# Fused cosformer attention and quick-GELU MLP on one core: d_ff units dealt by fours, w_in in three tiles, w_out in 8 KB pieces, and k^T v of the next batch set behind the last group of the first product

## The chip, the cores and the metric

The kernel runs on one core of one Trainium2 chip, in one launch. The metric is the device time of a run in microseconds (us). The times given before are 295.08, 295.93 and 295.89 us, median 295.89 us. The execution that the profiler recorded took 295.09 us; from its first to its last instruction it spans 293.4 us. The granted TensorE clock in it is 0.997 of full speed.

## The reference

For each of 8 batches and 8 heads (sequence 576, head dimension 64) the reference computes a linear attention, then puts the heads side by side and runs a two-layer MLP with 512 inputs and 2048 hidden units (d_ff). Cut to what matters:

```python
def phi(x, c, s):                      # c, s: cos and sin of pi/2 * position / S
    r = np.maximum(x, 0.0)
    return np.concatenate([r * c, r * s], axis=-1)
q_p, k_p = phi(q, cos_w, sin_w), phi(k, cos_w, sin_w)
kv = np.einsum('bhsf,bhsd->bhfd', k_p, v)
num = np.einsum('bhsf,bhfd->bhsd', q_p, kv)
den = np.einsum('bhsf,bhf->bhs', q_p, k_p.sum(axis=2))[..., None] + 1e-06
x = (num / den).transpose(0, 2, 1, 3).reshape(B * S, H * D)     # 4608 x 512
h = x @ w_in                                                    # 512 x 2048
g = h * (1.0 / (1.0 + np.exp(-1.702 * h)))
out = g @ w_out                                                 # 2048 x 512
```

The order in which the 2048 hidden units are numbered does not matter to the result, as long as w_in's columns and w_out's rows are numbered alike.

## The kernel before

**The MLP.** The hidden units are cut into 16 groups of 128 (`fc` 0 to 15). The first product of a batch, `mm1(b, fc)` (L281, matmuls on L273), makes one group for 512 of the batch's 576 tokens: four matmuls, one for each 128 rows of w_in (`kc`). The stationary operand (the weights that TensorE loads ahead of a matmul) is a slice of w_in, 128 columns that lie side by side in SBUF; the moving operand is x transposed. ScalarE applies the GELU from PSUM to a tile `g` (L278). The second product, `mm2(b, t, lo, hi)` (L317, matmuls on L322), goes the other way round: for each of four blocks of 128 tokens, `g` is the stationary operand and rows of w_out move, over the groups `lo` to `hi`. ScalarE copies the result out (L326), and GpSimd's queue stores it (L329).

**The last 64 tokens of each batch** are kept apart in `xt`. For batches 0 and 1 they are done together (`mm1_tail_first`, L290, called for b = 0 and b = 1): two calls for each batch, 32 matmuls of 64 columns on L294 in each call, 128 in all, each with its own load of 128 columns of w_in. For the six later batches they wait for the end (`mm1_tails`, L298, 64 matmuls of 384 columns on L301).

**`start_block`** (L342) opens batches 0 and 1: its first four groups are done in pieces of 128 tokens, as soon as these are there, so that 128 of the matmuls on L273 have 128 columns; each loads its own 128 columns of w_in.

**The attention** of the next batch is woven into the MLP of this one. `trig` (L140, VectorE on L147) makes `kr`, the features of k; `vcopy` (L162, VectorE on L168) makes `vt`, v in bf16; `trig_q` and `qturn_dma` make the features of q and transpose them by DMA. `kv_mm` (L203, L208) multiplies k^T v in 72 small matmuls, `kv_evac` (L211, L213) copies the result to SBUF (`kvs`) on VectorE, and `num_mm` and `num_div` (L217 and L225) use it, one block of tokens between two pieces of `mm2`.

**Order.** The schedule is written out by hand: each engine takes its instructions in the order in which the program names them, and waits where one is not ready. In the loop over batches from 1 (L460) the next batch's `trig_q` come at the first group, its `trig`, its `vcopy` and the loads of the batch after it (`load_next`, on SyncE's queue) at the second; and ahead of group 15 stand these lines:

```python
            if nb is not None and fc == 15:
                kv_open()
                kv_mm(0, 4, vt_rhs, 0, 65)
                kv_evac(0, 4)
            mm1(b, fc)
```

For b = 1 the two `mm1_tail_first` calls (L482, L483) and `mm2(1, 4, 0, FC)` (L484) follow the loop over the groups; then, as for every batch, `mm2` of the four token blocks, with the next batch's `num_mm` after each eight matmuls. Batch 1's own k^T v stands in the stage of batch 0 (L437 to L439), which the change does not touch.

**Weights.** w_in is one tile of 128 x 4 x 2048 bf16, filled by four DMAs of 512 columns each (L118); w_out is one tile filled by four DMAs of four groups each (L127). All eight are issued by GpSimd's queue, which also converts from float32. In HBM a run of 512 columns of w_in is 2 KB; so is a row of w_out. Between these loads the same queue issues batch 1's k, q and v (L413 to L419). A DMA of this queue waits for the eighth before it, since eight semaphores are used in turn.

Of the kernel before, what the change touches and what calls it, by code (L numbers as in the profile page):

```python
# [10 lines left out]
BF16 = mybir.dt.bfloat16  # L11
# [8 lines left out]
def kernel(  # L20
# [9 lines left out]
    nc = tc.nc  # L30
    B, H, S, D = q.shape
    d_model = H * D
    d_ff = moe_w_in.shape[1]
    KC = d_model // 128
# [6 lines left out]
    one = ctx.enter_context(tc.tile_pool(name="one", bufs=1))  # L41
# [13 lines left out]
    def src_of(src, b, i0=0, i1=NI):  # L55
        return src[b, 2 * i0:2 * i1].rearrange("(i hh) (p j) d -> (hh p) i (j d)", hh=2, j=NS)
# [39 lines left out]
    qn0 = qn.rearrange("p c h f -> p (c h f)")[:, 0:NS * NI * 128].rearrange(  # L96
        "p (j i f) -> p j i f", j=NS, i=NI)
    qT = one.tile([128, H, 640], BF16, name="qT")
    w_in_sb = one.tile([128, KC, d_ff], BF16, name="w_in_sb")
    w_out_sb = one.tile([128, FC, d_model], BF16, name="w_out_sb")  # L100
    nc.gpsimd.memset(vt[:, :, :, 64:66], 1.0)
    nc.gpsimd.memset(qT[:, :, S:640], 0.0)


    win_r = moe_w_in.rearrange("(kc p) f -> p kc f", p=128)
    wout_r = moe_w_out.rearrange("(fc p) d -> p fc d", p=128)

    def load(t, src, b, eng=nc.gpsimd):
        eng.dma_start(out=t, in_=src_of(src, b))
# [4 lines left out]
        eng.dma_start(out=qf[0:64, 2048:2560].rearrange("p (h e) -> p h e", h=H),  # L114
                      in_=q[b, :, 512:S, :].rearrange("h p d -> p h d"))

    def load_win(f0, f1):
        nc.gpsimd.dma_start(out=w_in_sb[:, :, f0:f1], in_=win_r[:, :, f0:f1])  # L118

    def load_next(b):  # L120

        load_q(b, nc.sync)
        load(kf, k, b, nc.sync)
        load(vf, v, b, nc.sync)

    def load_wout(g):
        nc.gpsimd.dma_start(out=w_out_sb[:, ts(g, 4), :], in_=wout_r[:, ts(g, 4), :])  # L127

    gate = const.tile([1, 4], F32)
    nc.gpsimd.tensor_copy(gate[0:1, 0:1], kf[0:1, 0, 0:1])  # L130
    for i in (0, 2):
        nc.gpsimd.dma_start(out=vb[:, i:i + 2], in_=src_of(v, 0, i, i + 2))
    load_win(0, 512)
    load_win(512, 1024)
    nc.gpsimd.tensor_copy(gate[0:1, 1:2], vb[0:1, 3, 0:1])
    load_win(1024, 1536)
    load_win(1536, 2048)


    def trig(dst, src, j, act=False):  # L140
        i = src[:, :, ts(j, 64)]
        for cs, w in enumerate((cosw, sinw)):
            o = dst[:, j, :, ts(cs, 64)]
            if act:
                nc.scalar.activation(o, i, AF.Relu, scale=w[:, j:j + 1])  # L145
            else:
                nc.vector.tensor_scalar(o, i, 0.0, w[:, j:j + 1], op0=MAX, op1=MUL)  # L147

    def trig_q(c, act=False):
        n = 128 if c < 4 else 64  # L150
        if c < 4:
            i = qf[:, 0:2048].rearrange("p (h c d) -> p c h d", h=H, c=4)[:, c]
        else:
            i = qf[0:64, 2048:2560].rearrange("p (h d) -> p h d", h=H)
        for cs, w in enumerate((cosw, sinw)):
            o, sc = qn[0:n, c, :, ts(cs, 64)], w[0:n, NS + c:NS + c + 1]
            if act:
                nc.scalar.activation(o, i, AF.Relu, scale=sc)
            else:
                nc.vector.tensor_scalar(o, i, 0.0, sc, op0=MAX, op1=MUL)  # L160
# [27 lines left out]
    def qturn_dma(c):  # L188
        n = 128 if c < 4 else 64
        nc.sync.dma_start_transpose(out=qT[:, :, c * 128:c * 128 + n],  # L190
                                    in_=qn[0:n, c].rearrange("p h f -> p (h f)"))
# [3 lines left out]
    def kv_open(i0=0, i1=NI):  # L195
        t = pat.tile([128, 2, 512], F32, name="at")
        for i in range(i0, i1):
            st["kv", i] = t[:, :, ds((i - i0) * 65, 65)]
        st["ps", i0] = t[:, :, 0:(i1 - i0) * 65]
        if i0 == 0:  # L200
            st["kvs"] = small.tile([128, 2, NI, VW], BF16, name="kvs", bufs=2)

    def kv_mm(i0, i1, rhs, col, n):  # L203
        for i in range(i0, i1):
            for j in range(NS):
                for hh in range(2):
                    r = slice(hh * 64, hh * 64 + 64)
                    nc.tensor.matmul(st["kv", i][:, hh, ds(col, n)], kr[r, j, i, :], rhs(r, i, j),  # L208
                                     start=(j == 0), stop=(j == NS - 1))

    def kv_evac(i0, i1):  # L211
        o = st["kvs"][:, :, i0:i1, 0:65]
        nc.vector.tensor_copy(o, st["ps", i0].rearrange("p hh (i e) -> p hh i e", e=65))  # L213
# [23 lines left out]
    x = {}  # L237
# [29 lines left out]
    hp = {}  # L267

    def mm1_part(b, fc, t0, t1):
        if t0 == 0:  # L270
            hp[fc] = pmm.tile([128, MT], F32, name="mm")
        for kc in range(KC):
            nc.tensor.matmul(hp[fc][:, t0:t1], w_in_sb[:, kc, ts(fc, 128)], x[b][:, kc, t0:t1],  # L273
                             start=(kc == 0), stop=(kc == KC - 1))

    def gelu(fc):
# [4 lines left out]
    def mm1(b, fc):  # L281
        mm1_part(b, fc, 0, MT)
        gelu(fc)
# [3 lines left out]
    xt = one.tile([128, KC, B * 64], BF16, name="xt")  # L287
    gt = one.tile([128, FC, B * 64], BF16, name="gt")

    def mm1_tail_first(b, half):  # L290
        hps = pmm.tile([128, 8, 64], F32, name="mm")
        for f in range(8):
            for kc in range(KC):
                nc.tensor.matmul(hps[:, f], w_in_sb[:, kc, ts(half * 8 + f, 128)], xt[:, kc, ts(b, 64)],  # L294
                                 start=(kc == 0), stop=(kc == KC - 1))
        nc.scalar.activation(gt[:, ts(half, 8), ts(b, 64)], hps, AF.Gelu_apprx_sigmoid)

    def mm1_tails(fc):  # L298
        hps = pmm.tile([128, MT], F32, name="mm")
        for kc in range(KC):  # L300
            nc.tensor.matmul(hps[:, 128:B * 64], w_in_sb[:, kc, ts(fc, 128)], xt[:, kc, 128:B * 64],  # L301
                             start=(kc == 0), stop=(kc == KC - 1))
        nc.scalar.activation(gt[:, fc, 128:B * 64], hps[:, 128:B * 64], AF.Gelu_apprx_sigmoid)

# [3 lines left out]
    def rows(b, t):  # L308

        if t == 4:  # L310
            return [(64 * u, 64, out_j[NS - 1] if b + u == 1 else out[(b + u) * S - 64:(b + u) * S])
                    for u in range(2)]
        if b == 0:
            return [(64 * u, 64, out_j[2 * t + u]) for u in range(2)]
        return [(0, 128, out[b * S:b * S + 512].rearrange("(p c) d -> c p d", c=4)[t])]

    def mm2(b, t, lo, hi, c0=0, c1=d_model, last=False):  # L317
        if lo == 0:
            yp[b, t, c0] = pmm.tile([128, d_model], F32, name="mm")
        for fc in range(lo, hi):  # L320
            w = gT[fc][:, ts(t, 128)] if t < 4 else gt[:, fc, ts(b // 2, 128)]
            nc.tensor.matmul(yp[b, t, c0][:, c0:c1], w, w_out_sb[:, fc, c0:c1],  # L322
                             start=(fc == 0), stop=(fc == FC - 1))
        if hi == FC:
            ysb = ypool.tile([128, d_model], F32, name="ysb")
            nc.scalar.activation(ysb[:, c0:c1], yp[b, t, c0][:, c0:c1], AF.Identity)  # L326
            for p0, n, dst in rows(b, t):
                eng = nc.sync if last else nc.gpsimd
                eng.dma_start(out=dst[:, c0:c1], in_=ysb[p0:p0 + n, c0:c1])  # L329
# [130 lines left out]
    for b in range(1, B):  # L460
        nb = b + 1 if b + 1 < B else None
        f0 = 5 if b == 1 else 0
        for fc in range(f0, FC):
            if nb is not None and fc == f0:
                for c in range(5):
                    trig_q(c)
                    qturn_dma(c)
            if nb is not None and fc == f0 + 1:
                for j in range(NS):
                    trig(kr, kf, j)  # L470
                vcopy(0, 4)
                if nb + 1 < B:
                    load_next(nb + 1)
            if nb is not None and fc == 15:
                kv_open()
                kv_mm(0, 4, vt_rhs, 0, 65)
                kv_evac(0, 4)
            mm1(b, fc)
        if nb is not None:
            x_open(nb)  # L480
        if b == 1:
            mm1_tail_first(1, 0)  # L482
            mm1_tail_first(1, 1)  # L483
            mm2(1, 4, 0, FC)  # L484
        if nb is None:
            for fc in range(FC):
                mm1_tails(fc)
            for u in range(3, B, 2):
                mm2(u, 4, 0, FC)
        for t in range(4):  # L490
            last = nb is None and t == 3
            if last:
                mm2(b, t, 0, FC, 0, 256)
                mm2(b, t, 0, FC, 256, 512, last=True)
                continue
            mm2(b, t, 0, 8)
            if nb is not None and t < 3:
                num_mm(2 * t)
                num_div(2 * t)
                xturn_dma(nb, 2 * t)  # L500
            mm2(b, t, 8, 16)
            if nb is not None and t < 2:
                num_mm(2 * t + 1)
                num_div(2 * t + 1)
                xturn_dma(nb, 2 * t + 1)
# [30 lines left out]
```

## Time and profile before

| what | value |
|---|---|
| runs shown | 295.08, 295.93, 295.89 us; median 295.89 us |
| profiled execution | 295.09 us, span 293.4 us (1.7 us lie around the span) |
| TensorE (PE) busy | 283.6 us, 97% of the span |
| VectorE (DVE), ScalarE (ACT) busy | 123.7 us (42%), 128.6 us (44%) |
| matmuls of the second product, L322 | 592, 512 columns but for 32 of 256 |
| matmuls of the first product, L273 | 480 of 512 columns, 128 of 128 columns |
| tails of batches 0 and 1, L294 | 128 of 64 columns |
| tails of batches 2 to 7, L301 | 64 of 384 columns |
| w_in and w_out loads | 4 and 4 DMAs of 512 KB (as bf16), median 9.9 and 17.6 us from issue to landing |

In the profile PE is TensorE's matmul side and PEld its weight loads, which run beside the matmuls. Matmuls are pipelined, so the duration of one in the profile is longer than the distance to the next: 512 columns are listed with a mean of 379 ns, but four of them, one group, take 0.86 us. Where costs are worked out, distances from start to start are used and not durations.

### The profile page before, as it was taken

The numbers are of one execution on the slowest core, as the hardware profiler recorded it, in microseconds if no ns is written. First come the engines' busy times: TensorE is split into PE (matmuls) and PEld (weight loads), VectorE is DVE, ScalarE is ACT, GpSimd is POOL, SyncE is SP. The second block draws the span as 40 slices with busy tenths as digits, with TensorE's granted clock in tenths as the row PEclk, the third lists the DMA queues.
The fourth block names the chain that finished last, engine by engine and source line by source line (L and its number), as shares of the span: only waits on it lengthen the run. The fifth ranks groups of instructions, "written<-read, shape, count | busy, mean of one in ns | idle before, by whom it ended". The sixth has DMA issues, their size and how long they took to land.

```text
span 293.4 us, 6032 instructions
## 1 busy us (share of the span) xinstructions
PE 283.6 (97%) x2461; PEld 148.6 (51%) x2461; DVE 123.7 (42%) x355; ACT 128.6 (44%) x224; POOL 58.9 (20%) x71
## 2 busy tenths in 40 slices
PE   8889999989999999999999999999999999999992
PEld 3674556736544454445544554455445544564452
DVE  4764514871379037903691269225931510000000
ACT  7957724762115711572147214631364136771111
POOL 6351004100216001600151014301340110001211
PEclk9999999999999999999999999999999999999998
DMA  7999999999979965997499859895840430001311
GB/s 253 240 220 275 354 164 208 387 231 239 385 151 187 287 252 137 190 268 278 128 173 241 313 143 157 226 346 131 151 104 2 99 97 30 1 0 37 72 72 72
DMA packets 74795, 53.54 MB, mean 182 GB/s; under 512 B 52624, under 2 KB 65552, under 8 KB 74768
## 3 DMA queue, kind: packets, MB, share of 16 engines
q1 hardware_dynamic: 66160, 35.53, 49.2%
q0 software_dynamic: 8608, 17.63, 23.0%
q8 instruction: 19, 0.31, 0.4%
q14 instruction: 8, 0.07, 0.1%
HBM read 36.70 MB, written 9.44 MB: 157 GB/s over the span
## 4 chain that ended last, share of the span: by engine, by line
PE 87%; DMA 6%; DVE 3%; SPq 1%; ACT 1%; issue 0%; ACTq 0%
PE mm L322 41%; PE mm L273 33%; DMA kf<-in_k_dram 6%; PE at L208 4%; PE mm L301 4%; PE at L221 3%; DVE kr L147 2%; PE mm L294 1%; ACT kr L145 1%; PE mm L176 1%; DVE xn L233 1%; DVE vt L168 0%; SPq L190 0%; PE at L250 0%; SPq L114 0%
## 5 line engine op out<-in xcount | busy, mean ns | idle before, releaser
L322 PE MATMUL mm<-w_out_sb,g 128*128 128x512 bf16 (+1 forms) x528 | 117.4, 372 | 0.0
L273 PE MATMUL mm<-xT,w_in_sb 128*128 128x512 bf16 (+1 forms) x608 | 114.5, 345 | 0.0
L278 ACT ACTIVATE g<-mm 128x512 bf16<-128x512 f32 x128 | 75.5, 598 | 41.4 <-PE mm L273 41.4
L329 POOL DMA_DIRECT2D out_dram<-ysb x44 | 46.4, 1057 | 217.3 <-ACT ysb L326 217.1
L273 PEld LDWEIGHTS <-w_in_sb 128*128 128x128 bf16 x608 | 53.7, 98 | 55.3
L322 PEld LDWEIGHTS <-g 128*128 128x128 bf16 x528 | 49.2, 98 | 50.9
L326 ACT ACTIVATE ysb<-mm 128x512 f32<-128x512 f32 (+1 forms) x37 | 21.7, 585 | 107.7 <-PE mm L322 107.7
L233 DVE TENSOR_TENSOR xn<-at,inv 128x512 bf16<-128x512 f32 x40 | 27.7, 691 | 1.4
L147 DVE TENSOR_SCALAR kr<-kf,cosw 128x256 bf16<-128x256 f32 x68 | 23.5, 346 | 10.6 <-DMA kf<-in_k_dram 10.6
L213 DVE CAST kvs<-at 128x520 bf16<-128x520 f32 (+1 forms) x9 | 5.8, 642 | 49.1 <-PE at L208 49.0
L229 DVE TENSOR_SCALAR den<-at 128x8 f32<-128x8 f32 x40 | 6.7, 166 | 44.2 <-PE at L221 44.2
L147 DVE TENSOR_SCALAR kr<-kf,sinw 128x256 bf16<-128x256 f32 x68 | 23.7, 348 | 0.0
L221 PEld LDWEIGHTS <-qT 128*128 128x128 bf16 x320 | 14.6, 97 | 7.3
L160 DVE TENSOR_SCALAR qn<-qf,cosw 128x512 bf16<-128x512 f32 (+1 forms) x33 | 15.8, 479 | 3.3 <-DMA qf<-in_q_dram 3.3
L221 PE MATMUL at<-kvs,qT 128*128 128x65 bf16 x320 | 16.0, 193 | 0.0
L160 DVE TENSOR_SCALAR qn<-qf,sinw 128x512 bf16<-128x512 f32 (+1 forms) x33 | 15.8, 480 | 0.0
L322 PE MATMUL mm<-w_out_sb,gt 128*128 128x512 bf16 x64 | 14.1, 379 | 0.0
L208 PEld LDWEIGHTS <-kr 64*128 64x128 bf16 x648 | 10.3, 94 | 5.5 <-issue 4.5
L301 PE MATMUL mm<-xt,w_in_sb 128*128 128x384 bf16 x64 | 10.6, 326 | 0.0
L208 PE MATMUL at<-vt,kr 64*128 64x65 bf16 x504 | 8.8, 190 | 1.6 <-DVE vt L168 1.6
L322 PEld LDWEIGHTS <-gt 128*128 128x128 bf16 x64 | 6.2, 98 | 7.2
L168 DVE CAST vt<-vf 128x2304 bf16<-128x2304 f32 (+1 forms) x7 | 8.9, 1265 | 0.8 <-DMA vf<-in_v_dram 0.8
(57 smaller groups left out, 99.3 us busy)
## 6 DMA issues: line engine op xcount, KB each, us to landing
kf<-in_k_dram SPq DMA_DIRECT2D x6, 1152.0 KB, 9.2
vf<-in_v_dram SPq DMA_DIRECT2D x6, 1152.0 KB, 11.7
out_dram<-ysb POOLq DMA_DIRECT2D x27, 256.0 KB, 2.7
qf<-in_q_dram SPq DMA_DIRECT2D x6, 1024.0 KB, 6.8
out_dram<-ysb POOLq DMA_DIRECT2D x17, 128.0 KB, 6.0
w_in_sb<-in_moe_w_in_dram POOLq DMA_DIRECT2D x4, 512.0 KB, 9.9
w_out_sb<-in_moe_w_out_dram POOLq DMA_DIRECT2D x4, 512.0 KB, 17.6
kf<-in_k_dram POOLq DMA_DIRECT2D x1, 1152.0 KB, 12.4
```

The source lines that it names most:

```text
L147: nc.vector.tensor_scalar(o, i, 0.0, w[:, j:j + 1], op0=MAX, op1=MUL)
L160: nc.vector.tensor_scalar(o, i, 0.0, sc, op0=MAX, op1=MUL)
L168: nc.vector.tensor_copy(o, i)
L208: nc.tensor.matmul(st["kv", i][:, hh, ds(col, n)], kr[r, j, i, :], rhs(r, i, j), start=(j == 0), stop=(j == NS - 1))
L221: nc.tensor.matmul(ps[:, h // 4, ds((h % 4) * 65, 65)], qT[:, h, ts(c, 128)], st["kvs"][:, hh, i, 0:65], start=True, stop=True)
L233: nc.vector.tensor_tensor(xn, pv[:, :, :, 0:64], inv.unsqueeze(3).to_broadcast([128, 2, 4, 64]), op=MUL)
L273: nc.tensor.matmul(hp[fc][:, t0:t1], w_in_sb[:, kc, ts(fc, 128)], x[b][:, kc, t0:t1], start=(kc == 0), stop=(kc == KC - 1))
L278: nc.scalar.activation(g, hp.pop(fc), AF.Gelu_apprx_sigmoid)
L301: nc.tensor.matmul(hps[:, 128:B * 64], w_in_sb[:, kc, ts(fc, 128)], xt[:, kc, 128:B * 64], start=(kc == 0), stop=(kc == KC - 1))
L322: nc.tensor.matmul(yp[b, t, c0][:, c0:c1], w, w_out_sb[:, fc, c0:c1], start=(fc == 0), stop=(fc == FC - 1))
L326: nc.scalar.activation(ysb[:, c0:c1], yp[b, t, c0][:, c0:c1], AF.Identity)
L329: eng.dma_start(out=dst[:, c0:c1], in_=ysb[p0:p0 + n, c0:c1])
```

## The change

Three edits, of which the first two belong together.

1. **The units are dealt by fours.** Group `fc = 4 g + c` now holds the hidden units 512 g + 4 p + c, for p from 0 to 127, instead of 128 neighbours. For w_out this means that partition p takes four neighbouring rows of HBM, 8 KB in one run, instead of four rows of 2 KB each that lie 128 rows apart. For w_in the layout in SBUF stays as it was, but the stationary operand of one matmul is now every fourth column (`wcol`): 128 bf16 values at a step of 8 bytes.
2. **w_in lies in three tiles** of 512, 512 and 1024 columns, each filled by one DMA. The third DMA takes the place of two, with runs of 4 KB in HBM.
3. **k^T v of the next batch** moves, in the loop over the batches 1 to 6, from ahead of `mm1(b, 15)` to behind it; for b = 1 also to behind the two `mm1_tail_first` calls.

The numbers of instructions on TensorE, VectorE, ScalarE and SyncE stay as they were, and on VectorE, ScalarE and SyncE their order too. GpSimd's queue has one DMA fewer.

```diff
-    w_in_sb = one.tile([128, KC, d_ff], BF16, name="w_in_sb")
+    w_in_t = [one.tile([128, KC, n], BF16, name=f"w_in_{i}") for i, n in enumerate((512, 512, 1024))]
...
-    wout_r = moe_w_out.rearrange("(fc p) d -> p fc d", p=128)
+    wout_r = moe_w_out.rearrange("(g p c) d -> g p c d", p=128, c=4)
...
-    def load_win(f0, f1):
-        nc.gpsimd.dma_start(out=w_in_sb[:, :, f0:f1], in_=win_r[:, :, f0:f1])
+    def load_win(i, f0):
+        n = w_in_t[i].shape[2]
+        nc.gpsimd.dma_start(out=w_in_t[i], in_=win_r[:, :, f0:f0 + n])
+
+    def wcol(kc, fc):
+
+        g, c = divmod(fc, 4)
+        w = w_in_t[g][:, kc, :] if g < 2 else w_in_t[2][:, kc, ts(g - 2, 512)]
+        return w.rearrange("p (f c) -> p f c", c=4)[:, :, c]
...
-        nc.gpsimd.dma_start(out=w_out_sb[:, ts(g, 4), :], in_=wout_r[:, ts(g, 4), :])
+        nc.gpsimd.dma_start(out=w_out_sb[:, ts(g, 4), :], in_=wout_r[g])
...
-    load_win(0, 512)
-    load_win(512, 1024)
+    load_win(0, 0)
+    load_win(1, 512)
     nc.gpsimd.tensor_copy(gate[0:1, 1:2], vb[0:1, 3, 0:1])
-    load_win(1024, 1536)
-    load_win(1536, 2048)
+    load_win(2, 1024)
...
-            nc.tensor.matmul(hp[fc][:, t0:t1], w_in_sb[:, kc, ts(fc, 128)], x[b][:, kc, t0:t1],
+            nc.tensor.matmul(hp[fc][:, t0:t1], wcol(kc, fc), x[b][:, kc, t0:t1],
                              start=(kc == 0), stop=(kc == KC - 1))
...
-                nc.tensor.matmul(hps[:, f], w_in_sb[:, kc, ts(half * 8 + f, 128)], xt[:, kc, ts(b, 64)],
+                nc.tensor.matmul(hps[:, f], wcol(kc, half * 8 + f), xt[:, kc, ts(b, 64)],
...
-            nc.tensor.matmul(hps[:, 128:B * 64], w_in_sb[:, kc, ts(fc, 128)], xt[:, kc, 128:B * 64],
+            nc.tensor.matmul(hps[:, 128:B * 64], wcol(kc, fc), xt[:, kc, 128:B * 64],
...
-            if nb is not None and fc == 15:
-                kv_open()
-                kv_mm(0, 4, vt_rhs, 0, 65)
-                kv_evac(0, 4)
             mm1(b, fc)
         if nb is not None:
             x_open(nb)
         if b == 1:
             mm1_tail_first(1, 0)
             mm1_tail_first(1, 1)
+        if nb is not None:
+            kv_open()
+            kv_mm(0, 4, vt_rhs, 0, 65)
+            kv_evac(0, 4)
+        if b == 1:
             mm2(1, 4, 0, FC)
```

## The prediction

> **What bounds the kernel now.** I read the page first, then the chain of waits in order of time, the list of waits, and the groups of instructions by form. On the page TensorE is the full engine, and VectorE and ScalarE are under half:
>
> ```profile
> PE 283.6 (97%) x2461; PEld 148.6 (51%) x2461; DVE 123.7 (42%) x355; ACT 128.6 (44%) x224; POOL 58.9 (20%) x71
> ```
>
> So a change counts only if it closes a hole in TensorE's stream or makes the stream itself longer. The list of waits has one hole of size behind the start-up, and the chain of waits, cut to 60 to 76 us, shows where it lies (columns: start, length, what):
>
> ```profile
> PE at L208 <- DVE vt L168: 1.6, 1, 1.6
> ```
>
> ```profile
> 60.41 2.93 DVE kr L147 x11
> 63.34 0.23 issue
> 63.56 1.66 DVE kr L147 x6
> 65.23 1.28 DVE vt L168
> 66.50 0.04 issue
> 66.55 1.26 PE at L208 x72
> 67.81 0.97 PE mm L273 x4
> 68.78 1.87 PE mm L294 x64
> ```
>
> The reader is to see that in batch 1 the k^T v of batch 2 (L208) waits for `vt`, which VectorE finishes at 66.5 us, and that group 15 (L273) and the 64 tail matmuls (L294), which need no `vt`, stand queued behind it. From there to the end the chain is TensorE alone, so whatever is won at 66 us is won at the end. In the timeline the last matmul of group 14 starts at 64.57 and the first of L208 at 66.55: 1.98 us. The same step takes 0.31 us in batch 2 (101.69 to 102.00). The hole is **1.67 us**.
>
> The second view needed is that of the loads and matmuls of w_in by form (busy us, mean ns of one; then idle before):
>
> ```profile
> L294 PEld LDWEIGHTS <-w_in_sb 128*128 128x128 bf16 x128 | 4.0, 98 | 0.5
> L294 PE MATMUL mm<-xt,w_in_sb 128*128 128x64 bf16 x128 | 4.1, 193 | 0.0
> L273 PE MATMUL mm<-xT,w_in_sb 128*128 128x128 bf16 x128 | 8.3, 219 | 0.0
> ```
>
> The durations here are those of a pipeline; what counts is the distance. On L294, 64 matmuls, each with its own load, fill 1.87 us: one load and one matmul every 29.2 ns, although a load is listed with 98 ns. So loads overlap one another, and a load of 128 neighbouring columns takes no more than 29.2 ns of TensorE's time. A matmul of 128 columns follows the one before after 55 to 56 ns (timeline at 16.4 us), one of 512 after 216 ns, one of 384 after 162.5 ns (L301: 64 in 10.40 us).
>
> **k^T v moved.** No instruction is added; the order on VectorE, ScalarE and SyncE is the same, so only TensorE's own order changes. With the hole gone, group 15 starts at about 64.79 (64.57 plus 0.216), takes 4 x 0.216 = 0.86, the tails take 1.87, and the step to L208 0.1: TensorE comes to k^T v at 67.6 us, 1.1 us after `vt` is there. **Gain 1.67 us**, all on the path. What is late next: `kvs` is copied in 0.70 us (L213) and used by L221. In batch 1, 24 matmuls of 512 columns (5.18 us) stand between; in batches 2 to 6 group 15 no longer does, but eight matmuls of L322 (1.73 us) still do, 1.73 less 0.70 and about 0.1 for the step, so 0.9 us to spare. If that cover went, it would cost what is missing, five times. The GELU of group 15 now has 1.3 us more before its `g` is used. In batches 2 to 6 the move gains nothing: `vt` has no wait there, and the two steps into and out of L208 (about 0.09 us each) stay, one on each side.
>
> **w_in and w_out by other DMAs.** These weigh only where TensorE waits for them, and in the trace it does not. The issues narrowed to single ones give: w_in's third and fourth pieces, issued at 12.10 and 12.84, land after 8.6 and 10.2 us, at 20.7 and 23.1. Group 8 is first used at 25.0 (22.43 plus 12 matmuls of 0.216). As one DMA of both, all must be there by then: 1.9 us to spare, if the merged one ends where the fourth piece ended. The third w_out piece is tighter: issued at 20.98, landed after 19.3 us at 40.3, first used at 40.7 (33.79 plus 32 times 0.216); the fourth, at 44.2 (23.37 plus 20.9), is used from about 46. The order in GpSimd's queue is the same with one DMA less, v of batch 1 no longer waits 0.87 us for a w_in semaphore, and the third w_out piece waits for w_in's second piece and not its third. The busy share of the DMA engines is above 1 in this stretch (1.20 from 12 to 26 us, 1.22 from 26 to 42), so fewer, longer runs can only bring things forward or leave them; k came in at 1152 KB in 2.8 us (25.9 after 23.1) where a w_out piece took 2.4 to 3.9 us between landings. **I count 0**: no gain, as nothing waits for it, and between no loss and the loss of one piece's slot, 3.9 us less 0.4 to spare, so 3.5 us, if one w_out piece came a whole slot later.
>
> **Stationary operands at a step of four.** All 800 matmuls by w_in (608 on L273, 128 on L294, 64 on L301) now load every fourth column. No row of the trace shows a weight load with a step: the operands of all listed loads lie side by side. The lower end of the cost is 0: the load has the same 128 values, is issued as often, and cannot shorten a stream that runs at the matmuls' pace. The upper end is the row's own duration: if such loads no longer overlapped, each would hold TensorE for 98 ns. Then L294 costs 128 x (98 - 29.2) = 8.8 us and the 128-column matmuls of L273 128 x (98 - 56) = 5.4 us, in all **14.2 us**; matmuls of 384 and 512 columns still cover it (162.5 and 216 ns). In between, a load of twice the known bound, 58.4 ns, costs 128 x 29.2 = 3.7 us on L294 and 128 x 2.4 = 0.3 us on L273, **4.0 us**. I take 0, since the nearest row, the same load with the columns side by side, already fits under the shortest matmul of w_in, and that row is a bound from above: on L208, with one column moving, a pair of loads of 64 partitions goes by every 25 ns (timeline at 8.60 us: 56 loads in 0.77 us, the last of them 0.09).
>
> The Trainium skill has a rule for either side. "SBUF — State Buffer", section "Specifications (TRN2)", gives 16-byte lines that want two hits each for full bandwidth; a step of 8 bytes has exactly two, so by that page the cost is 0, with nothing to spare. "TensorE: Matmul & The Clock Gate", section "Weight-path perf modes — Fast Weight Load (FWL) and DoubleRow", says that the fast load reads 32 bits, two bf16, at a time; by an estimate from that, a step of four makes half of each read useless, and a load that was bound by its reads would take twice as long. The same table lists strided columns as allowed. No run here shows either yet.
>
> **The sum.** Against the profiled execution: 295.09 (span 293.4 and 1.7 around it) less 1.67 is 293.4 us. The runs shown have their median 0.8 us higher, at 295.89, which gives 294.2. Of the four executions before, two lie at 295.1 and two at 295.9, so I forecast the middle of the two, **293.8 us** (own range 292.9 to 294.6).
>
> **Rivals.**
>
> 1. *The stepped load takes about twice its bound* (the other side). Place: L294 in batches 0 and 1, and the short matmuls of `start_block`. Price 4.0 us, so 293.8 + 4.0 = 297.8. It decides from the point where it eats the 1.67 us: 1.67 / 128 = 13 ns, a load of 42 ns instead of 29.2. For it: 29.2 ns is a bound, the tails have no cover, and no stepped load is in the trace. Against it: the bound is not reached as far as the rows show.
> 2. *The stepped loads do not overlap at all*: 293.8 + 14.2 = 308.0 us. For it: the 98 ns of every row; against it: it needs a change of mode, not only of speed.
> 3. *A load a little longer*, 36 to 49 ns: between 0.9 and 2.5 us on L294, and the change comes out within 0.3% of before, 294.7 to 296.3.
> 4. *The change does not do what it says*: `vt` comes later by more than 1.1 us, and k^T v waits again. As VectorE's order and its inputs are as before, there is little for it: 295.1 to 295.9.
> 5. *A weight piece comes late* in the first 45 us: up to 3.5 us, 293.8 to 297.3. For it only the 0.4 us at 40.7; against it the longer runs.
>
> **How the numbers follow.** The forecast has 0.60, rival 1 has 0.15, rival 2 0.07, rival 3 0.08, rival 4 0.04, rival 5 0.06 (a third of it still faster). A measurement of this kernel can tell about 0.3%, 0.9 us, from no change. Faster by more: 0.60 and 0.02 of rival 5. Within: 0.08, 0.04 and 0.01. Slower by more: 0.15, 0.07 and 0.03. The range leaves out rival 2, and goes from 292.9, the lower profiled sum with half a microsecond for scatter, to 298.0, rival 1 and as little above.
>
> **What would show it.** In the profile after, the wait of L208 for `vt` is gone from the list of waits, L208 of batch 1 starts at about 67.6 us, behind L294, and the chain holds no VectorE piece after 60 us. L294 still takes 1.87 us for 64; 3.7 us would be rival 1, 6.3 us rival 2, with 128-column matmuls at 58 or 98 ns. The groups of 512 columns stay at 0.86 us; if they do not, the load costs more than any bound here and the forecast is wrong altogether. TensorE shows no wait for w_in or w_out between 20 and 47 us, and the last w_out piece lands before 44.2.

## The result and the profile after

The changed kernel takes **294.06 us** at the median (22 runs), the kernel before 295.42 us in the 22 runs beside it. The ratio is **0.9964, 95% interval 0.9949 to 0.998**: faster by about 1.1 us (0.6 to 1.5). The medians lie 1.36 us apart, the means 1.1, for six of the changed kernel's runs took 295.4 us or more (four of them at a mean granted clock of 0.989) and the other sixteen 293.9 to 294.5. The profiled execution took 294.29 us, with a span of 292.6.

The same views again. On the page, TensorE's weight loads are busier by 9 us and all else is as it was:

```profile
PE 284.0 (97%) x2461; PEld 157.6 (54%) x2461; DVE 123.6 (42%) x355; ACT 128.7 (44%) x224; POOL 57.5 (20%) x70
```

The list of waits of the changed kernel, TensorE alone. The line of L208 (now L214) waiting for `vt` is gone; what stays is the start-up:

```profile
PE at L256 <- DVE xn L239: 1.4, 2, 0.8
PE mm L340 <- DVE warm L76: 1.3, 1, 1.3
PE at L214 <- DVE kr L153: 0.3, 1, 0.3
PE at L214 <- ACT kr L151: 0.2, 1, 0.2
```

The chain of waits, again from 60 to 76 us, all of it TensorE:

```profile
59.81 6.69 PE mm L279 x31
66.50 2.13 PE mm L300 x64
68.62 1.19 PE at L214 x72
69.81 5.29 PE mm L328 x24
```

So k^T v stands behind the tails and waits for nothing: TensorE comes to it at 68.56 us, and `vt` is ready at 66.19. But the 64 tail matmuls (L294 before, L300 now) take 2.13 us where they took 1.87. The groups by form say where that comes from:

```profile
L300 PEld LDWEIGHTS <-w_in 128*128 128x128 bf16 x128 | 4.6, 118 | 0.4
L300 PE MATMUL mm<-xt,w_in 128*128 128x64 bf16 x128 | 4.6, 198 | 0.0
L279 PE MATMUL mm<-xT,w_in 128*128 128x128 bf16 x128 | 8.3, 219 | 0.0
L279 PE MATMUL mm<-xT,w_in 128*128 128x512 bf16 x480 | 105.2, 379 | 0.0
```

A stepped load is listed with 118 ns instead of 98, and in the timeline the tails follow each other every 33.3 ns instead of 29.2. The matmuls of 128 columns kept their 8.3 us.

**One thing of the profile is not the change's.** The first matmul of the first product starts at 16.89 us here and at 16.41 in the profile before:

```profile
16.89 1.06 PE L279 MATMUL mm<-xT,w_in 128*128 128x128 bf16 x16
```

```profile
16.41 1.05 PE L273 MATMUL mm<-xT,w_in_sb 128*128 128x128 bf16 x16
```

This delay stems from transfers that both kernels issue alike and ahead of any changed one: the second piece of k landed at 6.20 instead of 6.02, the last piece of v, which is on the chain of waits here, at 12.61 instead of 11.93. In the other profiles of the table below this start lies between 16.50 and 18.73, with no order by kernel. It falls at 18.6 and 18.7 where the granted clock fell to one half for 3.4 us within the start-up, and those executions took 295.5 and 295.6 us. To take the start-up out, I compare below the stretch from the first matmul of the first product to the last matmul of all, from start to start, read in one timeline of each kernel. The three kernels below that wait for no `vt` and keep the tails at 29.2 ns agree in it to 0.01 us. Where the wait stays (before, dealing alone, behind group 15 alone), the stretch also holds how late `vt` came in that one execution.

| kernel | first matmul of the first product, us | stretch to the last matmul, us | against before | time, ratio to before (95%) |
|---|---|---|---|---|
| before | 16.41 | 271.55 | | |
| **changed** | 16.89 | 270.34 | -1.21 | 294.06 us, 0.9964 (0.9949 to 0.998) |
| move alone | 18.59 | 269.82 | -1.73 | 293.86 us, 0.9946 (0.9928 to 0.9965) |
| dealing alone | 16.60 | 272.19 | +0.64 | 295.24 us, 0.9988 (0.9967 to 1.0009) |
| changed, dealt by twos | 16.50 | 269.81 | -1.74 | 293.58 us, 0.9931 (0.9907 to 0.9956) |
| changed, step of eight | 16.73 | 274.33 | +2.78 | 298.01 us, 1.0097 (1.0084 to 1.011) |
| changed, neighbouring columns | 18.73 | 269.82 | -1.73 | 293.56 us, 0.9956 (0.9943 to 0.997) |
| move to behind group 15 alone | 16.71 | 270.85 | -0.70 | 294.69 us, 0.9985 (0.9977 to 0.9994) |

### The profile page after: what moved, and what is told of

Its sections match the earlier page's. It is cut to its first block, busy times and chain, and to the rows that moved or that the text cites. A ratio compares the mean times of both kernels' runs of the same rounds, so it can differ in the third digit from the quotient of the medians.

```text
span 292.6 us, 6031 instructions
## 1 busy us (share of the span) xinstructions
PE 284.0 (97%) x2461; PEld 157.6 (54%) x2461; DVE 123.6 (42%) x355; ACT 128.7 (44%) x224; POOL 57.5 (20%) x70
## 4 chain that ended last, share of the span: by engine, by line
PE 93%; DMA 4%; DVE 1%; POOL 0%; issue 0%; ACT 0%; ACTq 0%
PE mm L328 43%; PE mm L279 38%; PE mm L307 4%; PE at L227 3%; PE at L214 3%; DMA vb<-in_v_dram 2%; PE mm L300 1%; DMA kf<-in_k_dram 1%; PE at L256 1%; DVE xn L239 1%; POOL vb L139 0%; DVE inv L237 0%; PE mm L182 0%; DVE den L235 0%; ACT ysb L332 0%
## 5 line engine op out<-in xcount | busy, mean ns | idle before, releaser
L328 PE MATMUL mm<-w_out_sb,g 128*128 128x512 bf16 (+1 forms) x528 | 117.4, 372 | 0.0
L279 PE MATMUL mm<-xT,w_in 128*128 128x512 bf16 (+1 forms) x608 | 113.5, 345 | 0.0
L279 PEld LDWEIGHTS <-w_in 128*128 128x128 bf16 x608 | 61.7, 113 | 49.1
L328 PEld LDWEIGHTS <-g 128*128 128x128 bf16 x528 | 48.8, 98 | 50.0
L227 PEld LDWEIGHTS <-qT 128*128 128x128 bf16 x320 | 14.5, 97 | 7.3
L227 PE MATMUL at<-kvs,qT 128*128 128x65 bf16 x320 | 15.9, 193 | 0.0
L328 PE MATMUL mm<-w_out_sb,gt 128*128 128x512 bf16 x64 | 14.2, 379 | 0.0
L214 PEld LDWEIGHTS <-kr 64*128 64x128 bf16 x648 | 10.3, 94 | 4.0 <-issue 3.1
L307 PE MATMUL mm<-xt,w_in 128*128 128x384 bf16 x64 | 10.6, 326 | 0.0
L328 PEld LDWEIGHTS <-gt 128*128 128x128 bf16 x64 | 6.2, 97 | 7.3
L307 PEld LDWEIGHTS <-w_in 128*128 128x128 bf16 x64 | 7.2, 113 | 3.3
```

The lines of the kernel that those rows point to most:

```text
L227: nc.tensor.matmul(ps[:, h // 4, ds((h % 4) * 65, 65)], qT[:, h, ts(c, 128)], st["kvs"][:, hh, i, 0:65], start=True, stop=True)
L279: nc.tensor.matmul(hp[fc][:, t0:t1], wcol(kc, fc), x[b][:, kc, t0:t1], start=(kc == 0), stop=(kc == KC - 1))
L307: nc.tensor.matmul(hps[:, 128:B * 64], wcol(kc, fc), xt[:, kc, 128:B * 64], start=(kc == 0), stop=(kc == KC - 1))
```

## The experiments

After the result there were two theories. **A**: the move wins the whole hole, and the stepped loads of the tails give part of it back. **B**: the move wins less than the hole, and the rest of the change is neutral. A third, **C**, has the transfers at fault.

**1. The move alone.** The kernel before with the lines of edit 3 and nothing else.

```diff
-            if nb is not None and fc == 15:
-                kv_open()
...
+        if nb is not None:
+            kv_open()
```

> The kernel before with k^T v moved alone (w_in in one tile with neighbouring columns, w_out in 2 KB runs). Theory A (the move wins the whole hole of 1.67 us, and the changed kernel gives 0.62 us of it back to the stepped loads of the 128 tail matmuls, 34.0 ns each instead of 29.2): 1.67 us below before, ratio 0.9943, so about 0.6 us below the changed kernel; the tail matmuls at 29.2 ns. Theory B (the move wins only about 1.0 us and the loads and transfers are neutral): ratio 0.9965, equal to the changed kernel.

Measured: ratio 0.9946 (0.9928 to 0.9965), stretch 1.73 us shorter. The time alone does not part A from B, whose values both lie in the interval; the stretch does. Of the 1.73 us, 1.67 are the hole; most of the rest is one step of L221 at 45.7 us, which took 95 ns in the profile before, where others take 30, and does not show here. The rows of this kernel show no idle time before the k^T v that used to wait, and the tails as before, at 29.2 ns:

```profile
L208 PE MATMUL at<-vt,kr 64*128 64x65 bf16 x504 | 8.8, 190 | 0.0
L294 PE MATMUL mm<-xt,w_in_sb 128*128 128x64 bf16 x128 | 4.1, 193 | 0.0
```

Theory B falls: the move wins the whole hole of that profile, and the changed kernel is 0.52 us behind the move alone.

**2. The dealing alone.** The changed kernel with k^T v put back ahead of group 15.

> The changed kernel with k^T v back at its old place: only the dealing by fours, the three tiles and the 8 KB runs are left. Theory A: the tails of batch 0 cost 0.31 us, but this lies ahead of the wait for vt and shortens it, so that only batch 1's 0.31 us shows: ratio 1.001, with the wait of k^T v still listed, at 1.2 to 1.7 us. Theory B: 1.000, tails and transfers cost nothing at the end. Theory C (the transfers delay the start by the 0.5 us that the profile of the changed kernel shows): the first mm1 matmul starts at about 16.9 us again instead of 16.4, and the ratio is 1.001 to 1.003.

Measured: ratio 0.9988 (0.9967 to 1.0009). Theory A's 1.001 lies just above the interval and theory B's 1.000 in it, but the twelve runs spread from 293.96 to 295.85 us, more than the theories differ, so the time parts nothing. The stretch is 0.64 us longer; it is read in the slowest of the twelve. I had expected batch 0's 0.3 us to shorten the wait for `vt`, yet the wait is still 1.7 us long.

```profile
PE at L214 <- DVE vt L174: 1.7, 1, 1.7
```

In this profile batch 2's k landed at 60.85 us instead of 60.38, so `vt` was later as well. The longer tails did not hold k up: it was issued at 48.67 us, against 48.68 before, and took 12.18 us to land instead of 11.70. How far `vt` moves by itself shows beside the changed kernel, whose program is the same up to there: `vt` is ready 50.35 us after the first matmul of the first product here (66.95 less 16.60) and 49.30 there (66.19 less 16.89). So the length of the hole differs by about 1 us between these two executions. Of the 0.64 us, 0.27 are the later `vt`, 0.26 batch 1's tails, and 0.10 a place that I had not counted: after the first matmul of group 15 behind k^T v the next one comes after 242 to 244 ns instead of 226 to 227, in six batches. In the changed kernel L328 stands there and keeps its 226 to 227.

Theory C gets no support: the first product starts at 16.60 us here, with all of the change's transfers in place.

**3. Dealt by twos.** The changed kernel with a step of 4 bytes in the loads, and 4 KB runs of w_out.

```diff
-    wout_r = moe_w_out.rearrange("(g p c) d -> g p c d", p=128, c=4)
+    wout_r = moe_w_out.rearrange("(g p c) d -> g p c d", p=128, c=2)
...
-        return w.rearrange("p (f c) -> p f c", c=4)[:, :, c]
+        w = w[:, ts(c // 2, 256)]
+        return w.rearrange("p (f c) -> p f c", c=2)[:, :, c % 2]
...
-        nc.gpsimd.dma_start(out=w_out_sb[:, ts(g, 4), :], in_=wout_r[g])
+        nc.gpsimd.dma_start(out=w_out_sb[:, ts(g, 4), :].rearrange("p (g c) d -> p g c d", c=2), in_=wout_r[2 * g:2 * g + 2].rearrange("g p c d -> p g c d"))
```

> The changed kernel with the units dealt by twos: a step of 4 bytes in the weight loads, w_out in 4 KB runs, all else the same. If a load slows down with the number of 16-byte pieces of SBUF that it touches beyond some rate (16 for neighbours, 32 at a step of two, 64 at a step of four), a step of two costs less than a step of four, perhaps nothing: tail matmuls back at 29.2 ns, ratio to before 0.9943. If it slows down because half of each 32-bit read is useless, a step of two wastes as much as a step of four: tail matmuls at 33.3 to 34.0 ns, ratio 0.9964, as the changed kernel.

Measured: 293.58 us, ratio 0.9931 (0.9907 to 0.9956); one of its ten runs took 1693 us and is left out of the ratio. The stretch is 269.81 us, to 0.01 us that of the move alone. The groups by form of this kernel:

```profile
L301 PEld LDWEIGHTS <-w_in 128*128 128x128 bf16 x128 | 4.0, 98 | 0.5
L301 PE MATMUL mm<-xt,w_in 128*128 128x64 bf16 x128 | 4.1, 193 | 0.0
```

These are the rows of the kernel before, 98 and 193 ns. By the reading with the 32-bit reads a step of two would cost as much as a step of four, and it costs nothing that can be seen here. So useless halves are not what slows the step of four. This kernel has the lowest ratio of the study; against the move alone the intervals overlap, so what it shows is the whole of the move's gain with the dealing kept, and not a gain of its own.

**4. The load by itself, first try.** Behind batch 0's tails, for each of six steps, 32 loads with a matmul of 2 columns.

```diff
+    def every(step):
+        f = w_in_t[2].rearrange("p k f -> p (k f)")[:, 0:128 * step]
+        return f.rearrange("p (f c) -> p f c", c=step)[:, :, 0]
...
+    w = pmm.tile([128, 512], F32, name="mm")
+    for _ in range(32):
+        nc.tensor.matmul(w[:, 0:2], every(4), warm[:, 0:2], start=True, stop=True)
...
```

> The changed kernel with work added behind the tails of batch 0: for steps of 1, 2, 4, 8, 16 and 32 columns, 32 weight loads of 128 columns each with a matmul of 2 columns, so that the load alone sets the pace; then steps of 1, 8 and 16 with matmuls of 128 columns. It adds some 9 to 20 us that have no use. Expected at a step of 4: 33.3 ns from one to the next, as in the tails. If lines of 16 bytes set the pace: steps 1 and 2 at 25 ns or less, step 8 and above clearly slower than step 4 (about double, 60 to 70 ns), and flat from 8 on, where each value has a line of its own. If the 32-bit read sets it: step 2 equal to step 4 and to all above, 33.3 ns. With 128 columns (55.8 ns) steps whose load is under 55.8 ns show nothing.

Measured, from one to the next: 25, 25, 33, 60, 62 and 58 ns for steps of 1, 2, 4, 8, 16 and 32. The one run took 310.14 us. But from 36.7 us on the granted clock was 0.50, so that the last three steps and the first of the 128-column ones were read at half clock; with the clock back at 1.00, the 128-column matmuls at a step of 16 came every 62 ns. So the load of step 16 shows the same distance at either clock.

**5. The load by itself, with the clock kept up.** Eleven steps, and twelve matmuls of 512 columns ahead of each.

> The changed kernel with work added behind the tails of batch 0, none of it of use: for steps of 1, 2, 3, 4, 5, 6, 7, 8, 12, 16 and 32 columns, 32 weight loads of 128 columns with a matmul of 2 columns each, and twelve matmuls of 512 columns ahead of each step so that the clock stays up. If the pace follows the number of 16-byte pieces touched, at about 0.52 ns each: 25 ns (the least distance) for steps 1 to 3, 33 for 4, 42 for 5, 50 for 6, 58 for 7, 62 to 67 from 8 on. If a load needs two hits on each piece for full pace: 25 ns to step 3, and steps 5 to 7 as slow as step 8, 62 ns.

Measured, at a granted clock of 1.00 throughout. The rows of the timeline for steps 1 and 2 (L439, L443), 3 to 8 (L447 to L467), 12, 16 and 32; columns are start and length of the 32:

```profile
37.12 0.94 PE L439 MATMUL mm<-warm,w_in 128*128 128x2 bf16 x32
...
40.52 0.94 PE L443 MATMUL mm<-warm,w_in 128*128 128x2 bf16 x32
...
43.91 0.99 PE L447 MATMUL mm<-warm,w_in 128*128 128x2 bf16 x32
...
47.34 1.20 PE L451 MATMUL mm<-warm,w_in 128*128 128x2 bf16 x32
...
50.99 1.41 PE L455 MATMUL mm<-warm,w_in 128*128 128x2 bf16 x32
...
54.85 1.61 PE L459 MATMUL mm<-warm,w_in 128*128 128x2 bf16 x32
```

```profile
58.91 1.82 PE L463 MATMUL mm<-warm,w_in 128*128 128x2 bf16 x32
...
63.18 2.04 PE L467 MATMUL mm<-warm,w_in 128*128 128x2 bf16 x32
...
67.67 2.04 PE L471 MATMUL mm<-warm,w_in 128*128 128x2 bf16 x32
...
72.15 2.08 PE L475 MATMUL mm<-warm,w_in 128*128 128x2 bf16 x32
...
76.68 1.93 PE L479 MATMUL mm<-warm,w_in 128*128 128x2 bf16 x32
```

To get the distance, take the last matmul off (163 ns at a step of 1, 172 at 4, 198 at 8) and divide by 31: 25, 25, 27, 33, 40, 46, 53, 59, 59, 61 and 56 ns. The step of 4 gives the 33 ns of the tails, by the load alone. A step of s columns spreads 128 values over 16 s pieces of 16 bytes, up to 128 at a step of 8. From step 3 to step 8 each further step adds 6.6 ns for 16 more pieces, **0.41 ns a piece**, and from 8 on nothing more is added. The number of pieces was varied by the step alone, so that it is the pieces that cost is a reading that fits the line and its end at 8, and is not shown apart from other things that grow with the step. By that line a step of 2 would need 20 ns and neighbours 14, which the least distance of 25 ns hides. There is no jump between 4 and 5, so the rival reading, full pace up to two hits on a piece and a slow one beyond, does not hold; nor does the 32-bit read, which would set 2 equal to 4 where 25 and 33 ns are measured. My 0.52 ns a piece was too much, since it left no fixed part.

**6. A step of eight in the kernel.** The same tiles and transfers, weights from the flat row.

```diff
-        return w.rearrange("p (f c) -> p f c", c=4)[:, :, c]
+        w = w_in_t[min(g, 2)].rearrange("p k f -> p (k f)")[:, 0:1024]
+        return w.rearrange("p (f c) -> p f c", c=8)[:, :, 4 * (kc % 2) + c]
```

> The changed kernel with weight loads at a step of eight columns, 16 bytes (taken from the flat row of the tile, so that the weights are not those of the reference; all instructions, sizes and transfers as in the changed kernel). If the pace of a load follows the 16-byte pieces that it touches, as the first probe showed (33.3 ns at a step of four, 62 ns at steps of eight and sixteen), the 128 tail matmuls come every 62 ns, and the 128 matmuls of 128 columns every 62 ns instead of 56; those of 384 and 512 columns do not change. Against the kernel with the move alone that is 128 x (62 - 29.2) = 4.2 us and 128 x 6 = 0.8 us more: ratio to before 1.0112. If instead loads are slowed for another reason in the probe (the lower clock in part of it), the tails stay near 34 ns and the ratio near 0.997.

Measured: ratio 1.0097 (1.0084 to 1.011), just below the 1.0112 expected. The chain of waits of this kernel, the tails of batch 0:

```profile
29.84 2.81 PE mm L279 x13
32.65 3.95 PE mm L300 x64
36.60 3.45 PE mm L328 x16
```

64 tails in 3.95 us, 61.7 ns each (59.8 in batch 1). Against neighbouring columns (experiment 7) the stretch is 4.5 us longer: the tails account for 4.0 and the 128-column matmuls for 0.5. The latter were expected at 0.8; they take 0.6 more, and 0.16 of that comes off the steps from L227 to L256, where TensorE waits for `xn` anyway. The 512-column matmuls keep their 216 ns, the 384-column ones their 162.5. So the side on which this change could have failed is real, one more factor of two in the step away.

**7. The transfers without the steps.** The changed kernel with neighbouring columns in the loads.

```diff
-        return w.rearrange("p (f c) -> p f c", c=4)[:, :, c]
+        return w[:, ts(c, 128)]
```

> The changed kernel with its transfers (w_in in three tiles, w_out in 8 KB runs) and the moved k^T v, but weight loads of neighbouring columns (w_in's units then do not match w_out's, so the values are not the reference's). If the transfers neither win nor lose and the stepped loads are all that was given back: from the first matmul of the first product to the last matmul 269.8 us as in the kernel with the move alone, against 270.3 in the changed kernel; ratio to before 0.9943. If the transfers cost the time: 270.3 us and 0.9964.

Measured: ratio 0.9956 (0.9943 to 0.997), an interval that holds both expected values; the stretch decides: 269.82 us, that of the move alone to 0.01 us. Within the stretch the three tiles and the 8 KB runs neither win nor cost, and the 0.52 us between the move alone and the changed kernel are the stepped loads. What the transfers do ahead of the stretch this profile cannot say, since the clock fell in its start-up. The others whose clock did not fall start the first product at 16.41 and 16.71 us with the old transfers and between 16.50 and 16.89 with the new ones, so theory C has nothing for it beyond this scatter.

**8. Only half of the cover.** The kernel before with k^T v behind group 15, but ahead of the tails.

```diff
-            if nb is not None and fc == 15:
-                kv_open()
-                kv_mm(0, 4, vt_rhs, 0, 65)
-                kv_evac(0, 4)
             mm1(b, fc)
         if nb is not None:
             x_open(nb)
+        if nb is not None:
+            kv_open()
+            kv_mm(0, 4, vt_rhs, 0, 65)
+            kv_evac(0, 4)
         if b == 1:
             mm1_tail_first(1, 0)
```

> The kernel with the move alone, but for batch 1 k^T v stands behind group 15 and still ahead of the two tail calls. If the gain is the work that TensorE does in place of waiting, group 15's 0.86 us covers half of the hole: a wait of L208 for vt of about 0.75 to 0.8 us stays, the stretch from the first matmul of the first product to the last matmul is 270.6 to 270.7 us, and the ratio is about 0.997. If the place behind group 15 alone made the gain, the wait is gone and the stretch 269.8 us.

Measured: ratio 0.9985 (0.9977 to 0.9994); the 0.997 expected lies outside. The stretch is 270.85 us, 0.70 us shorter than before, and the wait is still listed:

```profile
PE at L208 <- DVE vt L168: 0.9, 1, 0.9
```

0.9 us of wait where 1.6 were. That it is 0.70 and not 0.86 is again `vt`, ready 50.25 us after the first matmul of the first product (66.96 less 16.71) where it was 50.08 before (66.49 less 16.41). The gain is what TensorE does in place of waiting: group 15 covers its 0.86 us and the tails are needed for the rest.

## Why the prediction was right

**The hole and the move: right, to 0.07 us.** Forecast 1.67 us, measured 1.73 with the move alone, and k^T v starts at 68.56 us in the changed kernel, which is, to 0.05 us, the 67.6 forecast plus the later start (0.48) and the longer tails (0.53). Experiment 8 shows the mechanism: with half of the work in the hole, half of the wait is left. But both numbers are measured against the one profile from which the forecast was taken. The hole's length is a matter of when `vt` comes, which differed by about 1 us between two executions that run the same program up to there (experiment 2); over the runs, the move alone is worth 1.6 us by its ratio and 1.42 by the medians.

The cover behind it held as forecast: in batch 2 `kvs` is copied by 104.15 us and first used at 105.07, 0.92 us to spare where 0.9 were counted, though group 15 no longer stands between.

**The transfers: right, at 0.** Experiment 7 shows it for the stretch. w_in's third piece landed at 22.97 us and was used at 25.5, the third w_out piece at 39.9 and was used at 41.5, the last at 43.2. What I argued beside it, that longer runs bring things forward, hardly shows: the four w_out pieces landed within 0.4 us of before, but for the last, 1.1 us earlier.

**The stepped loads: the mis-sized term.** "I take 0, since the nearest row, the same load with the columns side by side, already fits under the shortest matmul of w_in." The row was right and was no evidence for the stepped load: it bounds the load of neighbouring columns from above and says nothing of a load with a step. The stepped load takes 33.3 ns, 4.1 ns over the matmul of 64 columns; 128 x 4.1 is 0.52 us. That is the mechanism of rival 3, a load a little longer, below its range of 36 to 49 ns; rivals 1 and 2 priced the next steps, and experiment 6 came within 0.5 us of rival 1's price of 4.0. So the net is -1.2 and not -1.7 us, still faster by more than 0.3% by the ratio's middle, though its interval reaches down to 0.2%.

**The two rules on a load with a step.** The Trainium skill, "SBUF — State Buffer", section "Specifications (TRN2)", wants two hits on a 16-byte line for full bandwidth, and made the step of four free. Here it is not: 33.3 ns with two hits on each line, 27 with a step of three, and no change of slope at two hits. The same row says that each cross to a new line pays a penalty, which the prediction left out; a distance that grows by 0.41 ns with every further piece agrees with that half of it. The Trainium skill, "TensorE: Matmul & The Clock Gate", section "Weight-path perf modes — Fast Weight Load (FWL) and DoubleRow", has 32-bit reads; by the estimate from it, twice the time as soon as one half is useless, steps of two and of four would take the same, and they take 25 and 33 ns. Whether a step of two is any slower than neighbours the least distance of 25 ns hides.

**The absolute time** was forecast at 293.8 from four executions at 295.1 and 295.9. With the term above the sum is 294.3; measured 294.06. That 293.8 came within 0.3 us although 0.52 were left out is in part luck: the medians lie 1.36 us apart, the stretches of the two profiles 1.21.

## What to carry to other kernels

An engine that is 97% busy still has holes, and the worth of a move is the work it puts in a hole: find the wait in the chain, then count which queued instructions do not need what is waited for. For a resource that the trace shows only covered, the row is a bound and not a price: before a step, a stride or a size goes from the covered to the uncovered side, measure it alone, under the shortest instruction that it must hide behind. Where a layout has a free factor, as the dealing has here (steps of two, four and eight cost 0, 0.52 and 4.5 us), the smallest one that gives the transfers their long runs costs least on the engine's side, and it is worth asking whether anything waits for those transfers at all.

## What the runs showed of the hardware that I had not expected

- The distance between weight loads of 128 columns grows in a straight line with the step, and so with the 16-byte pieces touched, 0.41 ns each, from 27 ns (48 pieces) to 59 ns (128 pieces). It was 59 to 62 ns at steps of 8 and 16 with the granted clock at 0.50 as well as at 1.00.
- A step of 32 columns (64 bytes) is a little quicker than one of 16, 58 ns against 62 in the first probe and 56 against 61 in the second; why is open.
- Within the start-up the granted clock fell to one half for 3.4 us in the profiles of the move alone and of the neighbouring columns; the first product then began some 2 us later, at 18.6 and 18.7 us. Nothing here shows what sets it off.
